# A decode step of cached attention and a gated feed-forward: VectorE transposes keys and probabilities in 32x32 blocks, and w_down becomes one plain transfer

## The chip, the cores and the metric

The kernel runs on one core of a Trainium2 chip. TensorE (PE in the profile; PEld is its weight load) does the matmuls, VectorE (DVE), ScalarE (ACT) and GpSimd (POOL) the elementwise work, and SyncE (SP) issues nearly all transfers; 16 DMA engines carry them from HBM to the on-chip memory (SBUF). Matmuls write to PSUM. The metric is the device time of one execution in microseconds; three runs of the kernel before took 231.56 to 231.65 us, median 231.6.

## The reference

A parallel block for one new token in two sequences (B = 2). The layer norm of `x` feeds grouped-query attention over the last 4096 cached positions and a gated feed-forward; both are added to `x`.

```python
xn = _layernorm(x)                                   # x: 2 x 1 x 512
# attention: 32 query heads, 8 key heads (rep = 4), Dh = 128, W = 4096
q = (xn @ wq).reshape(B, 1, 32, 128)                 # wq: 512 x 4096
k, v = k_cache[:, :, Sk - W:, :], v_cache[:, :, Sk - W:, :]
p = softmax(q . k * Dh ** -0.5)                      # each key head for 4 query heads
attn = (p @ v).reshape(B, 1, 4096) @ wo              # wo: 4096 x 512
# feed-forward, F = 1792
gate, up = xn @ W_gate, xn @ W_up
gate = gate * (gate > 0)
return x + attn + (gate * up) @ W_down
```

All is float32. The two caches give 64 MiB of keys and values; with the weights 94.9 MB are read.

## The kernel before

The work is cut into groups g = 0 to 3 (two sets of four key heads times two sequences). A group has two `k` tiles and two `v` tiles, a = 0 and 1. A tile (`load_kv`, L114) holds two heads: 64 runs of 64 positions for each, so that partition 2 p + h has run p of head h, and 64 x 128 numbers lie in a partition, 4 MiB in all. Tiles and weights share a ring of four buffers (`ring`, L59). SyncE issues loads in program order, and each waits until the load four places ahead has been used up: `wq` in two parts, `w_gate`, `w_up`, then `k0_0`, `k0_1`, `k1_0`, `v0_0`, `k1_1`, `v0_1` and so on, at the end `v3_0`, `v3_1`, `w_down`, `wo` in two halves, the second in four pieces.

At the start x is normalised, q is computed in `q_ps`, transposed and put into `qz` (L143), which is zero but for the columns of the head that a matmul is for. Gate and up follow (`g_ps`, `u_ps`; the last 128 of 1792 columns in `x_ps`), and their product goes transposed into `hT`.

For a `k` tile, `transposes` (L308) turns 64 blocks of 128x128 on TensorE. Four land in one PSUM tile `pk`, and VectorE and ScalarE by turns copy it into `kT`, even and odd partitions (the two heads) apart. `scores` (L322) is eight matmuls a half tile, of 512 columns with 32 query columns each, over four 32-column groups of the array. `softmax` (L335) finds one maximum a head (reduction on VectorE, transpose on TensorE, reduction, and a matmul that spreads the negative maximum as the bias `nm`), takes the exponential on ScalarE into `p`, with each column twice, transposes `p` on TensorE (`pp`) and masks it into `pt`. `values` (L386) multiplies `pt` with a `v` tile into `o`; `gather` (L404) picks each head's part with four matmuls into `oa`; `finish` scales by the reciprocal sum `rl`. `spread_heads` puts heads in the layout `oT` for `wo`.

The order on each engine is the order of the program text; no scheduler changes it. `kwork` (L432) writes the transposes of the next tile between the steps of `softmax`, which is a generator for that, and holds scores back by half a tile (`pend`).

At the end, `project` (L478) multiplies rows of `w_down` and `wo` with `hT` and `oT`, four matmuls of 128 columns a row, one for each quarter of the output, all accumulating in `y_ps`. `w_down` (L95) comes as 13 rows a partition in one transfer, and the 128 rows left over as two transfers to 16 partitions each (`wx`), after POOL has cleared that tile.

Of the kernel before, what the change touches and what calls it, by code (L numbers as in the profile page):

```python
# [9 lines left out]
F32 = mybir.dt.float32  # L10
# [10 lines left out]
def kernel(  # L21
# [28 lines left out]
    S1 = W // (Q * 512)  # L50

# [10 lines left out]
    ps_kt = ctx.enter_context(tc.tile_pool(name="ps_kt", bufs=3, space=PSUM))  # L62
# [23 lines left out]
    FM = 13  # L86
    KX = 4
    LEFT = 0
    FX = F - P * FM
    RX = (FX - 8 * LEFT) // (8 * KX)  # L90
    SX = RX + (LEFT > 0)
    MQ = P * FM // Q
    assert 8 * KX * RX + 8 * LEFT == FX

    def load_down():  # L95
        t = ring.tile([P, FM, D], F32, name="wd", tag="ring")
        wx = ktp.tile([P, SX, D], F32, name="wx", tag="kT")
        nc.gpsimd.memset(wx[0:64], 0.0)  # L98
        nc.sync.dma_start(
            t.rearrange("p k e -> p (k e)"), w_down[0:P * FM, :].rearrange("(p k) e -> p (k e)", p=P)  # L100
        )
        row = P * FM
        for b in range(2):
            src = bass.AP(
                tensor=w_down.tensor, offset=w_down.offset + row * D,
                ap=[[RX * D, KX], [KX * RX * D, 4], [1, RX * D]],
            )
            nc.sync.dma_start(wx[32 * b:32 * b + 4 * KX, 0:RX].rearrange("p k e -> p (k e)"), src)
            row += 4 * KX * RX
        for i in range(LEFT):  # L110
            nc.sync.dma_start(wx[i:32:4, RX], w_down[row + 8 * i:row + 8 * i + 8, :])
        return t, wx
# [21 lines left out]
    for c0, c1 in ((0, 256), (256, 384), (384, 512)):  # L134
        nc.scalar.dma_start(x2[:, c0:c1], x[:, 0, c0:c1])  # L135
# [4 lines left out]

    NSLOT = C * S1
    qz = const.tile([P, NG, NSLOT * 36], F32, name="qz")
    nc.gpsimd.memset(qz, 0.0)  # L143
    ones = const.tile([1, 1], F32, name="ones")
# [4 lines left out]
    hT = const.tile([P, FM + SX, B, 16], F32, name="hT")  # L149
    nc.gpsimd.memset(hT, 0.0)  # L150
    hx = const.tile([32, SX, 64], F32, name="hx")
    nc.gpsimd.memset(hx, 0.0)
# [10 lines left out]
    for e in range(NE):  # L163
# [3 lines left out]
    pick = const.tile([P, 4, 24], F32, name="pick")  # L167
    nc.gpsimd.memset(pick, 0.0)
    nc.vector.tensor_reduce(
        out=pick[:, :, 8:16], in_=ident.rearrange("p (q u k) -> p u k q", q=Q, u=4), op=ALU.add, axis=AX.X  # L170
    )


    HK = 2 * REP
    by_h = const.tile([P, NP, HK], F32, name="by_h")
    nc.vector.tensor_reduce(
        out=by_h, in_=ident.rearrange("p (q a s k) -> p a k q s", q=Q, a=NP, s=S1), op=ALU.add, axis=AX.XY
    )

    half_of = const.tile([P, 2], F32, name="half_of")  # L180
    nc.vector.tensor_reduce(
        out=half_of, in_=ident.rearrange("p (y h) -> p h y", h=2), op=ALU.add, axis=AX.X
    )
    own = const.tile([P, 2, REP], F32, name="own")
    nc.vector.tensor_copy(own, half_of[:, :, None].to_broadcast([P, 2, REP]))
# [42 lines left out]
    for r in range(R):  # L228
# [3 lines left out]
        for i in range(REP):  # L232
            nc.tensor.transpose(
                qt[:, i].rearrange("p c s b -> p (c s b)"), qs[:, i * P:(i + 1) * P], ident
            )
        for b in range(B):
            dst = qz[:, r * B + b].rearrange("p (a s h k) -> p a s h k", a=NP, s=S1, h=2)
            for h in range(2):
                nc.vector.tensor_copy(
                    dst[:, :, :, h, 0:REP], qt[:, :, h::2, 0:S1, b].rearrange("p i a s -> p a s i")  # L240
                )
# [4 lines left out]
    x_ps = ps_1.tile([32, 2, FX], F32, name="x_ps", tag="o0")  # L246
    for h, dst, wt in ((0, g_ps, gw), (1, u_ps, uw)):
# [6 lines left out]
        for kc in range(KC):  # L254
            nc.tensor.matmul(
                x_ps[:, h], xnT[:, 1, kc, :], wt[:, kc, Q * MQ:], start=(kc == 0), stop=(kc == KC - 1)
            )
# [8 lines left out]
    )  # L266
    gx = work.tile([32, 2, FX], F32, name="gx", tag="qs")
    nc.scalar.copy(gx[:, 0], x_ps[:, 0])
    nc.vector.scalar_tensor_tensor(gx[:, 1], gx[:, 0], 0.0, gx[:, 0], op0=ALU.is_gt, op1=ALU.mult)
    part = 4 * KX * RX  # L270
    for b in range(2):
        g_in, u_in = (
            a[:, b * part:(b + 1) * part].rearrange("p (j e s) -> p e j s", j=4, e=KX) for a in (gx[:, 1], x_ps[:, 1])
        )
        nc.vector.tensor_tensor(
            hx[:, 0:RX, 32 * b:32 * b + 4 * KX].rearrange("p s (e j) -> p e j s", j=4), g_in, u_in, op=ALU.mult
        )
    for i in range(LEFT):
        lo = 2 * part + 8 * i
        nc.vector.tensor_tensor(  # L280
            hx[:, RX, i:32:4], gx[:, 1, lo:lo + 8], x_ps[:, 1, lo:lo + 8], op=ALU.mult
        )
    ht_ps = ps_1.tile([P, FM + SX, B], F32, name="ht_ps", tag="misc")
    for k in range(FM):
        for c in range(Q):
            nc.tensor.matmul(
                ht_ps[32 * c:32 * c + 32, k], hh[:, k], ident[:, 32 * c:32 * c + B], start=True, stop=True
            )
    for k in range(SX):
        m = 64 if k < RX else 32  # L290
        nc.tensor.matmul(ht_ps[0:m, FM + k], hx[:, k, 0:m], ident[0:32, 0:B], start=True, stop=True)
    nc.vector.tensor_copy(hT[:, 0:FM, :, 0], ht_ps[:, 0:FM])
    nc.vector.tensor_copy(hT[0:64, FM:FM + RX, :, 0], ht_ps[0:64, FM:FM + RX])
    if LEFT:
        nc.vector.tensor_copy(hT[0:32, FM + RX, :, 0], ht_ps[0:32, FM + RX])

    HW = W // S1
    ss, pts, rls = {}, {}, {}  # L300
    kts, osb = {}, {}
    turn = [0]

    def evacuate(dst, src):
        (nc.vector.tensor_copy if turn[0] % 2 else nc.scalar.copy)(dst, src)  # L305
        turn[0] += 1

    def transposes(g, a, s1, kt_in):  # L308

        kt = ktp.tile([P, 2, HW], F32, name=f"kT{g}_{a}_{s1}", tag="kT")  # L310
        kts[g, a, s1] = kt
        for n in range(2 * Q):
            pk = ps_kt.tile([P, 512], F32, name=f"pk{g}_{a}_{s1}_{n}", tag="kt")
            for u in range(4):
                j = 8 * Q * s1 + 4 * n + u
                nc.tensor.transpose(pk[:, u * P:(u + 1) * P], kt_in[:, j * P:(j + 1) * P], ident)  # L316
            evacuate(
                kt[:, :, n * 256:(n + 1) * 256], pk.rearrange("p (y h) -> p h y", h=2),
            )
            yield  # L320

    def scores(g, a, s1):  # L322
        if (a, s1) == (0, 0):
            ss[g] = ps_s.tile([P, 512], F32, name=f"s{g}", tag="s")
        kt = kts.pop((g, a, s1))
        for h in range(2):
            n = (a * S1 + s1) * 2 + h
            for q in range(Q):
                nc.tensor.matmul(  # L329
                    ss[g][32 * q:32 * q + 32, :], qz[:, g, 32 * n:32 * n + 32],  # L330
                    kt[:, h, q * 512:(q + 1) * 512],
                    start=(a == 0 and s1 == 0 and h == 0), stop=(a == NP - 1 and s1 == S1 - 1 and h == 1),
                )

    def softmax(g):  # L335
# [3 lines left out]
        yield  # L339
        mt = ps_1.tile([1, P], F32, name=f"mt{g}", tag="misc")  # L340
        nc.tensor.transpose(mt, m, ident)
        mx = work.tile([1, NP, HK], F32, name=f"mx{g}", tag="mx")
        nc.vector.tensor_reduce(
            out=mx, in_=mt.rearrange("p (q a s k) -> p a k q s", q=Q, a=NP, s=S1), op=ALU.max, axis=AX.XY
        )
        mb = work.tile([1, NP, S1, HK], F32, name=f"mb{g}", tag="mb")
        nc.vector.tensor_scalar(
            mb, mx[:, :, None, :].to_broadcast([1, NP, S1, HK]), -SCALE, None, op0=ALU.mult
        )
        yield  # L350
        nm_ps = ps_1.tile([P, 1], F32, name=f"nm_ps{g}", tag="misc")
        for q in range(Q):
            nc.tensor.matmul(
                nm_ps[32 * q:32 * q + 32, :], mb.rearrange("p a s k -> p (a s k)"), ones, start=True, stop=True
            )
        nm = work.tile([P, 1], F32, name=f"nm{g}", tag="nm")
        nc.vector.tensor_copy(nm, nm_ps)  # L357

        p = work.tile([P, 512, 2], F32, name=f"p{g}", tag="p", bufs=1)
        l = work.tile([P, 1], F32, name=f"l{g}", tag="l")  # L360
        both = ss[g][:, :, None].to_broadcast([P, 512, 2])
        nc.scalar.activation(p, both, AF.Exp, bias=nm, scale=SCALE, accum_out=l)  # L362
        yield
        yield
        yield

        pts[g] = work.tile([P, 2, Q * NP * S1, 4, HK], F32, name=f"pt{g}", tag="pt")
        pv = p.rearrange("r y h -> r (y h)")
# [163 lines left out]
```

## Time and profile before

| quantity | value |
|---|---|
| median of three runs | 231.6 us (231.56 to 231.65) |
| profiled execution | 231.43 us |
| its span, first to last instruction | 229.6 us |
| mean granted TensorE clock | 0.938 of full |
| read from HBM | 94.90 MB, 413 GB/s over the span |
| TensorE busy | 81%, 1876 matmul issues |
| VectorE busy | 29%, 135 instructions |

A float32 matmul appears as two issues with a weight load each; a transpose as one. In the page, a group's row has line, engine, operation, tile written and tiles read, shape and count; then busy us, mean ns of one; then idle time before and what ended it. In the chain of waits, each piece has start, length and what it was. A stretch of the table by windows has start and end, its length, busy time (and count) of PE, PEld, DVE, ACT and POOL, then the granted clock, the DMA share and GB/s. PE busy time counts pipelined matmuls from issue to end, so it isn't the share of the array's peak.

### The profile page before, as it was taken

How to read it: one execution, taken by the hardware profiler on the slowest of the kernel's cores; microseconds unless marked ns; L12 is line 12 of the kernel's file. 1: busy time of each engine (PE TensorE's matmuls, PEld its weight loads, DVE VectorE, ACT ScalarE, POOL GpSimd, SP SyncE). 2: the span in 40 equal slices, each digit the busy share in tenths (PEclk: the TensorE clock that was granted, in tenths of full speed). 3: DMA queues.
4: the chain of work that ended last, by engine and by line, in shares of the span. 5: the costliest groups of instructions: out<-in, count | busy, mean ns of one | idle time of the engine just before them, and what ended most of it. 6: DMA issues, size and time to landing. Idle time of an engine off the chain costs nothing.

```text
span 229.6 us, 4149 instructions
## 1 busy us (share of the span) xinstructions
PE 185.4 (81%) x1876; PEld 114.7 (50%) x1876; DVE 67.2 (29%) x135; ACT 46.9 (20%) x80; POOL 8.2 (4%) x25
## 2 busy tenths in 40 slices
PE   0059961779999899997799699889979973988794
PEld 0052231259666583663484566458446532247682
DVE  0320021034444570441472143157124224001000
ACT  0020100004344451440351233045023202010000
POOL 8100000000000000000000000000000300000000
PEclk9999999577999999999999799999999999599678
DMA  7999999999999999999999999999999999999981
GB/s 274 451 428 408 454 410 437 422 451 442 405 425 451 415 417 445 442 411 420 457 417 432 428 440 414 434 445 414 422 440 437 417 428 440 423 442 414 410 364 49
DMA packets 3824, 95.15 MB, mean 414 GB/s; under 512 B 434, under 2 KB 448, under 8 KB 704
## 3 DMA queue, kind: packets, MB, share of 16 engines
q1 hardware_dynamic: 3796, 94.90, 96.7%
q8 instruction: 14, 0.23, 0.4%
q14 instruction: 2, 0.02, 0.0%
q10 hardware_dynamic: 12, 0.00, 0.0%
HBM read 94.90 MB, written 0.00 MB: 413 GB/s over the span
## 4 chain that ended last, share of the span: by engine, by line
DMA 54%; PE 41%; DVE 2%; issue 1%; ACT 1%; ACTq 0%; POOL 0%; DVEq 0%
DMA k<-in_A_k_cache_dram 37%; PE pk L316 21%; DMA wo<-in_A_wo_dram 13%; PE s L329 7%; PE y_ps L480 5%; DMA x<-in_A_x_dram 4%; PE o L393 3%; PE q_ps L222 3%; PE xt_ps L212 2%; ACT p L362 1%; PE pp L373 0%; ACTq L135 0%; PE oa L409 0%; DVE stats L189 0%; DVE kT L305 0%
## 5 line engine op out<-in xcount | busy, mean ns | idle before, releaser
L316 PE MATMUL pk<-ident,k 128*128 128x128 f32 x512 | 67.9, 286 | 6.0 <-DMA k<-in_A_k_cache_dram 5.9
L316 PEld LDWEIGHTS pk<-ident,k 128*128 128x128 f32 x512 | 57.9, 146 | 20.9 <-issue 16.7
L305 DVE COPY kT<-pk 128x512 f32<-128x512 f32 x64 | 44.2, 691 | 52.1 <-PE pk L316 46.2
L305 ACT COPY kT<-pk 128x512 f32<-128x512 f32 x64 | 37.5, 585 | 69.5 <-PE pk L316 69.5
L393 PE MATMUL o<-v,pt 128*32 128x512 f32 x256 | 32.5, 641 | 0.0
L329 PE MATMUL s<-kT,qz 128*32 128x512 f32 x256 | 30.9, 598 | 0.0
L393 PEld LDWEIGHTS o<-v,pt 128*32 128x32 f32 x256 | 11.3, 117 | 15.7 <-issue 10.9
L212 PE MATMUL xt_ps<-rep,xn 2*128 2x32 f32 x16 | 3.7, 400 | 13.9 <-DVE xn L206 13.9
L329 PEld LDWEIGHTS s<-kT,qz 128*32 128x32 f32 x256 | 7.1, 109 | 11.9 <-issue 11.5
L305 DVE COPY on<-o 128x512 f32<-128x512 f32 x4 | 2.8, 692 | 30.5 <-PE o L393 30.5
L409 PE MATMUL oa<-on,pick 128*16 128x128 f32 x64 | 8.3, 273 | 4.1 <-DVE on L305 3.3
L480 PE MATMUL y_ps<-wo,oT 128*17 128x128 f32 x256 | 10.3, 329 | 1.6 <-DMA wo<-in_A_wo_dram 1.6
L409 PEld LDWEIGHTS oa<-on,pick 128*16 128x16 f32 x64 | 5.8, 97 | 11.3 <-DVE on L305 7.0
L250 PE MATMUL u_ps<-wu,xnT 128*32 128x416 f32 x32 | 5.8, 901 | 6.1 <-DMA wu<-in_B_W_up_dram 6.1
L212 PEld LDWEIGHTS xt_ps<-rep,xn 2*128 2x128 f32 x16 | 3.6, 320 | 13.9 <-issue 13.9
L222 PE MATMUL q_ps<-wq,xnT 128*32 128x512 f32 x64 | 9.7, 777 | 0.5 <-DVE xnT L214 0.5
L480 PEld LDWEIGHTS y_ps<-wo,oT 128*17 128x17 f32 x256 | 8.1, 119 | 3.6 <-DMA wo<-in_A_wo_dram 2.6
L305 ACT COPY on<-o 128x512 f32<-128x512 f32 x4 | 2.3, 586 | 27.0 <-PE o L393 27.0
L98 POOL MEMSET wx<- 64x2048 f32 x1 | 1.8, 1804 | 169.1 <-PE s L329 169.1
L362 ACT ACTIVATE p<-s,nm 128x1024 f32<-128x1024 f32 x4 | 4.5, 1114 | 13.1 <-DVE nm L357 13.1
L374 DVE TENSOR_TENSOR pt<-pp,own 128x512 f32<-128x512 f32 x8 | 5.4, 689 | 2.6 <-PE pp L373 2.6
L373 PE MATMUL pp<-ident,p 128*128 128x128 f32 x32 | 4.9, 280 | 1.7 <-ACT p L362 1.5
(83 smaller groups left out, 68.2 us busy)
## 6 DMA issues: line engine op xcount, KB each, us to landing
k<-in_A_k_cache_dram SPq DMA_DIRECT2D x8, 4096.0 KB, 23.9
v<-in_A_v_cache_dram SPq DMA_DIRECT2D x8, 4096.0 KB, 28.3
wq<-in_A_wq_dram SPq DMA_DIRECT2D x2, 4096.0 KB, 21.7
wo<-in_A_wo_dram SPq DMA_DIRECT2D x1, 4096.0 KB
wg<-in_B_W_gate_dram SPq DMA_DIRECT2D x1, 3584.0 KB, 29.8
wu<-in_B_W_up_dram SPq DMA_DIRECT2D x1, 3584.0 KB, 39.3
wd<-in_B_W_down_dram SPq DMA_DIRECT2D x1, 3328.0 KB
wo<-in_A_wo_dram SPq DMA_DIRECT2D x1, 2048.0 KB
```

Source lines behind the costliest of these rows:

```text
L212: nc.tensor.matmul(xt_ps[:, o, kc, :], cols, rep.rearrange("r s b -> r (s b)"), start=True, stop=True)
L222: nc.tensor.matmul(q_ps[r][32 * c:32 * c + 32, :], xnT[:, 0, kc, :], wqt[kc // 2][:, kc % 2, n * 512:(n + 1) * 512], start=(kc == 0), stop ...
L250: nc.tensor.matmul(dst[32 * c:32 * c + 32, :], xnT[:, 1, kc, :], wt[:, kc, c * MQ:(c + 1) * MQ], start=(kc == 0), stop=(kc == KC - 1),)
L305: (nc.vector.tensor_copy if turn[0] % 2 else nc.scalar.copy)(dst, src)
L316: nc.tensor.transpose(pk[:, u * P:(u + 1) * P], kt_in[:, j * P:(j + 1) * P], ident)
L329: nc.tensor.matmul(ss[g][32 * q:32 * q + 32, :], qz[:, g, 32 * n:32 * n + 32], kt[:, h, q * 512:(q + 1) * 512], start=(a == 0 and s1 == 0 ...
L362: nc.scalar.activation(p, both, AF.Exp, bias=nm, scale=SCALE, accum_out=l)
L373: nc.tensor.transpose(pp[:, u], pv[:, lo:lo + P], ident)
L374: nc.vector.tensor_tensor(pts[g][:, jh].rearrange("p n u k -> p u n k"), pp.rearrange("p u (n k) -> p u n k", k=HK), own.rearrange("p h i ...
L393: nc.tensor.matmul(o[32 * q:32 * q + 32, :], pts[g][:, jh, n].rearrange("p u k -> p (u k)"), v[:, lo:lo + 512], start=(s1 == 0 and jh == 0 ...
L409: nc.tensor.matmul(oa[g], pick[:, u, 8 - 8 * a:24 - 8 * a], ons[a][:, u], start=(a == 0 and u == 0), stop=(a == NP - 1 and u == 3),)
L480: nc.tensor.matmul(y_ps[32 * e:32 * e + 17, :], lhsT.rearrange("p b s -> p (b s)")[:, 0:17], w[:, e * P:(e + 1) * P], start=False, stop=stop,)
```

## The change

Keys are no longer transposed on TensorE. VectorE's block transpose turns each 32x32 block of a `k` tile where it stands, four instructions of 2048 columns a tile, from SBUF to SBUF. A head's 128 dimensions then come as four column blocks (`CB`), with 32 partitions for 32 rows, and the four partition blocks (`PB`) hold different positions. q is therefore block diagonal: `spot` copies a block of q to all partition blocks, and sixteen small copies a set, on VectorE and ScalarE, place it in `qz`. Scores are eight matmuls a half tile as before, but a half tile's go to two of the four 32-row parts of `s`. The heads of a tile are now a and a + 2.

`p` has 512 columns, each once. A matmul with a permutation (`perm`, one for each head of a tile) reorders its rows into `pp`, and one VectorE block transpose writes `pt`. `values` copies its result through a `mask` on VectorE, so that `gather` is one matmul of 512 columns, and `finish` adds four parts.

No tile's work is written between another's steps: a step is scores, maximum, values, softmax, gather, and the turning of `p`. At the end the rows of `w_down`, `wo0` and the first eight of `wo1` are one matmul of 512 columns each, over four column groups by turns, into `y4`; that is copied and folded into `y_ps`, and the last eight rows go as before. `w_down` is one transfer with 14 rows a partition. x comes in five pieces in place of three.

```diff
+    L = 32
+    PB = P // L
+    CB = DH // L
-    ps_kt = ctx.enter_context(tc.tile_pool(name="ps_kt", bufs=3, space=PSUM))
+    ps_kt = ctx.enter_context(tc.tile_pool(name="ps_kt", bufs=2, space=PSUM))
...
     def load_down():
         t = ring.tile([P, FM, D], F32, name="wd", tag="ring")
-        wx = ktp.tile([P, SX, D], F32, name="wx", tag="kT")
-        nc.gpsimd.memset(wx[0:64], 0.0)
...
+            t.rearrange("p k e -> p (k e)"), w_down.rearrange("(p k) e -> p (k e)", p=P)
+        )
+        return t
...
-        base = cache[b, r * C + 2 * a, SK - W:SK, :]
+        base = cache[b, r * C + a, SK - W:SK, :]
-            tensor=cache.tensor, offset=base.offset, ap=[[run, PK], [SK * DH, 2], [1, run]]
+            tensor=cache.tensor, offset=base.offset, ap=[[run, PK], [NP * SK * DH, 2], [1, run]]
...
-    for c0, c1 in ((0, 256), (256, 384), (384, 512)):
+    for c0, c1 in ((0, 256), (256, 320), (320, 384), (384, 448), (448, 512)):
...
+        for cb in range(CB):
+            nc.tensor.matmul(
+                rq[:, cb].rearrange("p b c i -> p (b c i)"), spot[:, cb].rearrange("p b e -> p (b e)"),
+                qT.rearrange("p b c i -> p (b c i)"), start=True, stop=True,
+            )
         for b in range(B):
+            for pb in range(PB):
+                rows = slice(L * pb, L * pb + L)
+                for a in range(NP):
+                    lo = 2 * a * 16 + pb * REP
+                    (nc.vector.tensor_copy if a else nc.scalar.copy)(
+                        qz[rows, r * B + b, :, :, lo:lo + REP], rq[rows, :, b, a::NP, :]
+                    )
...
+    def scores(g, a, kt_in):
+        if a == 0:
             ss[g] = ps_s.tile([P, 512], F32, name=f"s{g}", tag="s")
+        for s1 in range(S1):
+            kt = ktp.tile([P, CB, 2, JH, KL], F32, name=f"kT{g}_{a}_{s1}", tag="kT")
+            for n in range(2):
+                lo = JH // 2 * n
+                j = JH * s1 + lo
+                nc.vector.transpose(
+                    kt[:, :, :, lo:lo + JH // 2, :].rearrange("p c h j k -> p j c k h"),
+                    kt_in[:, j * DH:(j + JH // 2) * DH],
                 )
+            for cb in range(CB):
+                for h in range(2):
+                    lo = 32 * (2 * s1 + h)
+                    nc.tensor.matmul(
+                        ss[g][lo:lo + 32, :], qz[:, g, cb, h, 16 * a:16 * a + 32],
+                        kt[:, cb, h].rearrange("p j k -> p (j k)"),
+                        start=(a == 0 and cb == 0), stop=(a == NP - 1 and cb == CB - 1),
+                    )
...
+    def turn(g, p, l):
+        pp = ps_kt.tile([P, 2, 512], F32, name=f"pp{g}", tag="kt")
+        for h in range(2):
+            nc.tensor.matmul(pp[:, h], perm[:, h], p, start=True, stop=True)
+        pts[g] = work.tile([P, NP * S1, JH, HK], F32, name=f"pt{g}", tag="pt")
+        nc.vector.transpose(pts[g].rearrange("p n j k -> p j n k"), pp.rearrange("p h y -> p y h"))
...
+    for g in range(NG):
         for a in range(NP):
             kt_in = load_kv(k_cache, "k", g, a)
+            v_in = load_kv(v_cache, "v", g - 1, a) if g else None
+            scores(g, a, kt_in)
+            nm = maxima(g) if a else None
+            if g:
+                values(g - 1, a, v_in)
+            pl = softmax(g, nm) if a else None
+            if g:
+                gather(g - 1, a)
+                if a:
+                    finish(g - 1)
+                elif g % B == 1 and g > 1:
+                    spread_heads((g - 2) // B)
             if a:
+                turn(g, *pl)
...
+    def slot(lhsT, w):
+        t, i = done[0] % Q, done[0]
+        nc.tensor.matmul(
+            y4[32 * t:32 * t + 32, :], lhsT.rearrange("p b s -> p (b s)"), w, start=(i < Q), stop=(i >= EARLY - Q)
+        )
+        done[0] += 1
...
+            if j == cuts[1][1]:
+                ys = work.tile([P, D], F32, name="ys", tag="qs")
+                nc.vector.tensor_copy(ys, y4)
+                quarters(fold[:, 0:17], ys, False)
```

Three places show how instructions moved. A row has the line, the operation, the tile written (with group and a in its name), the tiles read, the shape and how many in a row. The first is VectorE between the scores of group 1 and the first tile of group 2. Before:

```order
L305 COPY kT1_1_1_788<-pk1_1_1_4_813 128x2x256
L305 COPY kT1_1_1_788<-pk1_1_1_6_825 128x2x256
L305 COPY on0_1_867<-o0_1_850 128x512
L418 TENSOR_SCALAR osb0_873<-oa0_845,rl0_673 16x128
L305 COPY kT2_0_0_879<-pk2_0_0_1_886 128x2x256
L338 TENSOR_REDUCE m1_906<-s1_699 128x1
L305 COPY kT2_0_0_879<-pk2_0_0_3_908 128x2x256
L343 TENSOR_REDUCE mx1_916<-mt1_914 1x16
```

The same place now:

```order
L294 STREAM_TRANSPOSE kT1_1_1_461<-k1_1_446 128x16x4x16x2 x2
L310 TENSOR_REDUCE m1_472<-s1_402 128x1
L314 TENSOR_REDUCE mx1_476<-mt1_474 1x16
L319 TENSOR_SCALAR mb1_478<-mx1_476 1x64 x2
L325 COPY nm1_483<-nm_ps1_481 128x1
L357 TENSOR_TENSOR on0_1_502<-o0_1_485,mask_120 128x512
L374 TENSOR_REDUCE su0_509<-oa0_444 16x128
L375 TENSOR_SCALAR osb0_508<-su0_509,rl0_396 16x128
L339 STREAM_TRANSPOSE pt1_515<-pp1_512 128x32x4x8
L343 RECIPROCAL rl1_519<-lp1_517 16x1
L294 STREAM_TRANSPOSE kT2_0_0_526<-k2_0_521 128x16x4x16x2 x2
```

The first tile of group 2 stood ahead of the maximum of group 1; now it stands behind the whole softmax of group 1 and the masked results `on` of the tile before.

On TensorE, the same group, before:

```order
L329 MATMUL s1_699<-kT1_1_0_731,qz_91 32x512 x8
L409 MATMUL oa0_845<-on0_0_725,pick_118 16x128 x4
L393 MATMUL o0_1_850<-v0_1_729,pt0_633 32x512 x16
L409 MATMUL oa0_845<-on0_1_867,pick_118 16x128 x4
L316 MATMUL pk2_0_0_0_880<-ident_86,k2_0_875 128x128 x4
L316 MATMUL pk2_0_0_1_886<-ident_86,k2_0_875 128x128 x4
L329 MATMUL s1_699<-kT1_1_1_788,qz_91 32x512 x8
```

And now:

```order
L301 MATMUL s1_402<-kT1_1_0_450,qz_93 32x512 x8
L301 MATMUL s1_402<-kT1_1_1_461,qz_93 32x512 x8
L312 MATMUL mt1_474<-ident_88,m1_472 1x128
L323 MATMUL nm_ps1_481<-ones_97,mb1_478 128x1
L352 MATMUL o0_1_485<-v0_1_448,pt0_392 32x512 x16
L365 MATMUL oa0_444<-on0_1_502,picks_124 16x512
L337 MATMUL pp1_512<-p1_504,perm_132 128x512 x2
```

The `pk` transposes, 64 a tile, are gone, and with them the work that stood between one step's results and the next.

The last place is TensorE's end, after the last `values`. Before:

```order
L480 MATMUL y_ps_1579<-wd_1538,hT_97 17x128 x52
L480 MATMUL y_ps_1579<-wx_1539,hT_97 17x128 x16
L423 MATMUL op1_1701<-osb1_1524,spread_108 128x32 x8
L480 MATMUL y_ps_1579<-wo0_1711,oT_101 17x128 x64
L480 MATMUL y_ps_1579<-wo1_1777,oT_101 17x128 x64
```

Now:

```order
L424 MATMUL y4_788<-wd_780,hT_101 32x512 x14
L380 MATMUL op1_847<-osb1_763,spread_110 128x32 x8
L424 MATMUL y4_788<-wo0_857,oT_103 32x512 x16
L424 MATMUL y4_788<-wo1_875,oT_103 32x512 x8
L431 MATMUL y_ps_782<-ys_888,fold_128 17x128 x4
L431 MATMUL y_ps_782<-wo1_875,oT_103 17x128 x32
```

One matmul of 512 columns stands where four of 128 stood, for all but the last eight rows of `wo`, and the fold stands between.

More of the change, by code (lines that the diff above doesn't have):

```diff
@@ L266 @@
     )
[L267 to L277, printed above, removed]
@@ L292 @@
[L292 to L295, printed above, removed]
+    ht_ps = ps_1.tile([32, FM * Q, B], F32, name="ht_ps", tag="misc")
+    firsts = ident.rearrange("p (c r) -> p c r", c=Q)[:, :, 0:B]
+    for k in range(FM):
+        nc.tensor.matmul(ht_ps[:, k * Q:(k + 1) * Q], hh[:, k], firsts, start=True, stop=True)
+    for c in range(Q):
+        nc.vector.tensor_copy(hT[32 * c:32 * c + 32, :, :, 0], ht_ps[:, c::Q])
@@ L299 @@
     HW = W // S1
+    JH = J // S1
+    KL = L // 2
     ss, pts, rls = {}, {}, {}
[L301 to L320, printed above, removed]
@@ L345, in softmax @@
         )
[L346 to L350, printed above, removed]
+        mb = work.tile([1, S1, C, PB, REP], F32, name=f"mb{g}", tag="mb")
+        for s1 in range(S1):
+            nc.vector.tensor_scalar(
+                mb[:, s1], mx[:, :, None, :].to_broadcast([1, C, PB, REP]), -SCALE, None, op0=ALU.mult
+            )
         nm_ps = ps_1.tile([P, 1], F32, name=f"nm_ps{g}", tag="misc")
[L352 to L355, printed above, removed]
+        nc.tensor.matmul(nm_ps, mb.rearrange("p s x b i -> p (s x b i)"), ones, start=True, stop=True)
@@ L364, in softmax @@
[L364 to L368, printed above, removed]
[L369 to L378 removed]
+        nc.scalar.activation(p, ss[g], AF.Exp, bias=nm, scale=SCALE, accum_out=l)
```

210 lines of the change are left out of this document (70 added, 140 removed).

## The prediction

> **What bounds the kernel now.** I read the page's slices first, then the table by stretches, then the chain of waits, and last the timeline around the places that the change rewrites.
>
> ```profile
> PE 185.4 (81%) x1876; PEld 114.7 (50%) x1876; DVE 67.2 (29%) x135; ACT 46.9 (20%) x80; POOL 8.2 (4%) x25
> DMA  7999999999999999999999999999999999999981
> q8 instruction: 14, 0.23, 0.4%
> ...
> 120.00:140.00 20.00, 17.93 (x142) 11.72 (x141) 6.87 (x12) 5.82 (x10) 0.00 (x0) 0.91 1.01 430
> ...
> 220.00:224.00 4.00, 4.00 (x128) 3.62 (x120) 0.00 (x0) 0.00 (x0) 0.00 (x0) 0.81 0.85 348
> 224.00:227.00 3.00, 2.56 (x76) 1.49 (x64) 0.29 (x1) 0.00 (x0) 0.00 (x0) 1.00 0.21 82
> ```
>
> The DMA row is full from the second slice to the last but one, and the stretch 120 to 140 moves 430 GB/s with all engines busy. PE at 81% looks close to a bound, but it is fed by the transfers: the chain steps from a matmul back to a landing again and again.
>
> ```profile
> 24.50 26.72 DMA k<-in_A_k_cache_dram
> 100.73 28.26 DMA k<-in_A_k_cache_dram
> 129.12 5.48 PE pk L316 x32
> 136.46 3.97 PE pk L316 x32
> 216.27 7.96 PE y_ps L480 x189
> 224.27 1.29 PE y_ps L480 x40
> 226.20 0.46 PE y_ps L480 x8
> 226.69 0.29 DVE yo L502
> ```
>
> The first `k` tile lands at 24.50 + 26.72 = 51.22 us, the sixth `k` tile at 128.99. Eight transfers of 4096 KB lie between: (128.99 - 51.22) / 8 = **9.72 us each**, 38.9 us for the four tiles of a group (two of `k`, two of `v`). So the kernel now runs as fast as data come; whatever the engines save inside the loop is worth nothing by itself. What can be gained lies after the last landing and in the ragged end of the transfers; what can be lost is a loop whose own length exceeds 38.9 us.
>
> **Is the new loop shorter than 38.9 us?** The old code interleaves `k` transposes of the next group with softmax, so no engine waits long. The new order is serial: VectorE transposes a `k` tile, TensorE multiplies, VectorE masks the result of `values`, and only then come the transposes of the next tile. I add up one group, from rows.
>
> ```profile
> L305 DVE COPY kT<-pk 128x512 f32<-128x512 f32 x64 | 44.2, 691 | 52.1 <-PE pk L316 46.2 <-ACT on L305 5.2
> L214 DVE COPY xnT<-xt_ps 128x256 f32<-128x256 f32 x1 | 0.4, 423 | 3.9 <-PE xt_ps L212 3.9
> L338 DVE TENSOR_REDUCE m<-s 128x1 f32<-128x512 f32 x4 | 2.8, 691 | 4.8 <-PE s L329 4.8
> L347 DVE TENSOR_SCALAR mb<-mx 1x32 f32<-1x32 f32 x4 | 0.7, 169 | 0.1
> 60.33 1.85 PE s L329 x16
> 195.47 6.37 PE L393 MATMUL o<-v,pt 128*32 128x512 f32 x32
> 189.19 0.69 DVE L338 TENSOR_REDUCE m<-s 128x1 f32<-128x512 f32 x1 [1.43 <-PE s L329]
> 191.36 1.11 ACT L362 ACTIVATE p<-s,nm 128x1024 f32<-128x1024 f32 x1 [11.38 <-DVE nm L357]
> 87.49 3.43 PE o L393 x32
> ```
>
> A *VectorE transpose* has no row. Two copies give the price of a column: (691 - 423) / 256 = 1.05 ns, with 155 ns fixed. A transpose of 128x2048 at one column a step is then 2048 x 1.05 + 155 = **2.30 us**. Below, two columns a step would make it 1.2 us; above, a transpose that passes each column twice would make it 4.4 us. I take 2.30, the row of the same engine, type and kind of work; the ends are rivals below.
> The Trainium skill speaks against that value: its page "VectorE: DVE Perf Modes", section "The three transpose paths", states 311 ns for a 128x128 bf16 block set. Sixteen such sets would be 4.98 us by it. No row of this trace shows a transpose on VectorE, so by that figure the third rival holds.
>
> *Scores*: a half tile was 16 issues (eight matmuls, two issues each) over four column groups of 32 in 1.85 us. One round of 512 columns takes 0.43 us (3.43 us for 32 issues of `o`, eight rounds of four). The new `scores` writes rows 32 (2 s1 + h), so only two groups work at a time: 16 issues are eight rounds and a drain, 3.6 us. The first half runs beside transposes three and four (4.6 us); the second half follows them. *Values*: `o`, 32 issues over four groups, 3.43 us and its drain, 3.6; with the masked copy (0.69, as the copies of 128x512 above) and hops, 4.5.
>
> - Step a = 0: four transposes 9.2, second half of scores 3.6, values and mask 4.5: **17.3 us**.
> - Step a = 1: 9.2 + 3.6; maximum to bias 191.36 - 189.19 = 2.17, with one more `mb` of 0.17, 2.35; values and mask 4.5; `oa`, two issues of 512 columns in one group, 0.86; the permutation `pp`, four full-width issues of 0.43, 1.72; its transpose of 1024 columns 1.23; hops 0.4: **23.9 us**. ACT's exponential lies beside `values`.
>
> That is 41.2 us at full clock, already 2.3 us over 38.9. The clock will not stay full. TensorE idles through the first two transposes of each step (4.6 us). Before, 32 `pk` issues took 5.48 us after a wait for `k`, against 3.97 us in the run that followed: 1.5 us lost, and the stretch 120 to 140 has a granted clock of 0.91. The `o` issues of 195.47 took 6.37 us instead of 3.6, 2.8 us lost. Between these, 2.15 us a step, of which 1.0 (4.6 - 3.6) is covered by transposes three and four: 1.15 a step, 2.3 a group. The gap in softmax (2.35 us) may cost another 0 to 2.8 us; I take nothing. **43.5 us a group.**
> The Trainium skill's page "TensorE: Matmul & The Clock Gate", Part 1, says that the clock halves after about one idle window of 3.4 us and returns after such a window of sustained work. By it the 4.6 us gaps cool the array and the softmax gap need not. The trace agrees on the halving and the order of the loss (1.5 and 2.8 us), though the wait at 129.12 was shorter than a window.
>
> **The sum to the end.** The second `k` tile lands at 51.22 + 9.72 = 60.9. Its transposes, scores with the cold start, bias, exponential (0.8), `pp`, transpose and hops are 9.2 + 4.75 + 2.35 + 0.8 + 1.7 + 1.2 + 0.5 = 20.5, so group 0 is done at 81.5. Three groups of 43.5 end at 212.0. Behind that stand, all with data landed:
>
> ```profile
> L480 PE MATMUL y_ps<-wd,hT 128*17 128x128 f32 x104 | 3.2, 273 | 0.0
> L423 PE MATMUL op<-osb,spread 16*128 16x32 f32 x32 | 3.9, 273 | 0.0
> ```
>
> Two `values` with mask and gather, 2 x (4.5 + 0.86) = 10.7; `wd` as 28 issues of 512 columns at 1.85 / 16 = 0.116 us, 3.25; `op` and its copy 2.25; `wo0` and the first eight rows of `wo1`, 48 issues, 5.55; the copy `ys` 0.9; `fold` and the last 64 issues, 72 at 3.2 / 104 = 0.03 us, 2.2; drain 0.3. In sum 25.1: `yo` starts at 237.1, against 226.69. From there the ends are alike (229.6 - 226.69 = 2.9): a span of 240.0. The profiled execution took 231.43 us beside its span of 229.6, 1.83 more, and the runs' median is 231.6: **241.7 us, say 241.5**.
>
> **Transfers in that picture.** A tile is loaded when the tile four loads earlier is used up, so the lag becomes late issues.
>
> ```profile
> 179.39 0.33 SPq L99 DMA_DIRECT2D wd<-in_B_W_down_dram  x1
> 185.58 18.08 SPq L498 DMA_DIRECT2D wo<-in_A_wo_dram  x5
> 1.58 8.89 DMA x<-in_A_x_dram
> wu<-in_B_W_up_dram SPq DMA_DIRECT2D x1, 3584.0 KB, 39.3
> ```
>
> `wd` waits for the last `k` tile: 212.0 - 43.5 + 17.3 + 1.15 + 9.2 = 196, 17 us later than now; `wo0` waits for `o` behind it, at 207. By then the queue has just run dry (two further tiles and `wd` are due at about 207), so `wo0` lands near 219 and `wo1`, issued at 216, near 229. TensorE reaches them at 228 and 232: late, but not what decides. The rest costs nothing while this holds. The plain `wd` (3584 KB in one transfer) replaces 3328 KB, two small transfers and POOL's memset in the same queue; the 128 KB pieces went away from where the queue is full. Two more pieces of `x` may double the 8.89 us wait of the layer norm, and sixteen small copies of `qz` add some 3 us before the gate matmuls; cover: loads are in flight until `wu` lands at 2.15 + 39.3 = 41.5, and the first `k` is not needed before 51.2. Fewer TensorE issues (1876 to 948) mean about 7 instruction packets instead of 14.
>
> **The rivals.**
>
> 1. *The transfers stay the bound* (the other side). If the loop is under about 40 us (a transpose nearer 2.0 us, or a clock that stays up), the lag never reaches the end: with three groups of L, `yo` starts at 81.5 + 3 L + 25.1, which meets today's 226.69 at L = 40.0. Then the end is the last landing. The ragged end (348 and 82 GB/s in 7 us, some 1.4 MB under the full rate, 3 us) can shrink with half the instruction packets and a balanced `wd`; I take 0.3 to 1.2 us of it, 230.6 us. For it speaks the full DMA row, against it the sum of 41.2 us without any cold start. Chance 0.20.
> 2. *Two column groups don't lift the clock.* Every warm-up in the trace came with four groups or full width. If two are too few, both score halves run at half rate, 7.2 us each: a step grows from 9.2 + 3.6 to 4.6 + 14.4, by 6.2, and cold `o` adds up to 2.8. L is 53.6 to 59; with 56, 87 + 168 + 25 + 2.9 + 1.83 = 285 us. Against it: nothing shows the clock counting groups. Chance 0.08.
> 3. *A transpose passes each column twice* (4.4 us). Eight a group add 17, and hide the cold starts: L = 58; with 9 more ahead, 90 + 174 + 25 + 2.9 + 1.83 = 294 us. Chance 0.04.
>
> **How the numbers follow.** The forecast has 0.68. Its own range: L moves by 8 us per us of transpose, and 2.15 to 2.5 us, with 0 to 2.8 for the softmax gap, gives 236 to 250. The first rival joins below, so the range is 230.4 to 250; the two dear rivals (0.12) are left out. A measurement of this kernel tells 0.2%, about 0.5 us, from no change. Of the first rival's 0.20 some 0.16 is faster by more than that and 0.04 within it; all else is slower, 0.80.
>
> **What would show it.** Right: 32 transposes near 2.3 us; VectorE busy near 100 us; a granted clock well under 0.94, low at the start of each score block; `k` issues drifting later by 4 to 5 us a group against their landings; DMA digits under 9 only in the last fifth; the chain alternating between VectorE transposes, `s` and `o`, with hardly any DMA at its end. Wrong: transposes of 1.2 or 4.4 us; `s` in 1.85 or 7 us; or a chain that still ends on `wo`, which is the first rival.

## The result, and the profile after

The changed kernel takes 278.69 us (median of six runs, 277.64 to 281.30), the kernel before 231.48 us (231.28 to 231.65) beside it: a ratio of 1.206, with a 95% interval of 1.199 to 1.213. The forecast was slower, but 241.5 us. The profiled execution took 277.64 us, with a span of 275.9 us. So the loss is 47 us and not 10.

From the page of the changed kernel: busy time, two rows of the slices, the instruction queue, and the chain that ended last, by engine and by line.

```profile
PE 166.6 (60%) x948; PEld 51.7 (19%) x948; DVE 147.2 (53%) x121; ACT 8.3 (3%) x27; POOL 8.1 (3%) x31
...
PEclk9999968859898559959995797799759957999999
DMA  7999999999999905996996289799907992999940
...
q8 instruction: 7, 0.11, 0.2%
...
DVE 48%; PE 41%; issue 6%; POOL 3%; ACT 1%; POOLq 0%; ACTq 0%
DVE kT L294 40%; PE o L352 10%; PE s L301 9%; PE q_ps L221 3%; PE pp L337 3%; PE y L424 3%; PE oa L365 2%; DVE pt L339 2%; PE g_ps L258 2%; DVE on L357 2%; PE op L380 1%; PE xt_ps L211 1%; PE u_ps L258 1%; PE rq L239 1%; DVE m L310 1%
```

The DMA row, which was full, has holes from the fifteenth slice on, and the chain, in which transfers had 54%, has none. It runs through VectorE and TensorE by turns, and 40% of the span is one line: the block transposes of the keys. TensorE is busy for 60% and VectorE for 53%. So the loop is now serial and longer than the transfers, as forecast; what differs is by how much.

The groups of instructions, with different shapes apart, show the two kinds of block transpose:

```profile
L294 DVE STREAM_TRANSPOSE kT<-k 128x2048 f32<-128x2048 f32 x32 | 115.6, 3722 | 0.0
...
L339 DVE STREAM_TRANSPOSE pt<-pp 128x1024 f32<-128x1024 f32 x4 | 5.0, 1250 | 7.0 <-PE pp L337 7.0
```

The second, of 1024 columns out of PSUM, takes 1.25 us, close to the forecast's 1.05 ns a column and 0.155 us (1.23 us). The first, of 2048 columns, should then take 2.3 us and takes 3.7 us. A group's place in the chain of waits (start, length, what):

```profile
86.75 3.21 PE pp L337 x4
...
91.27 14.39 DVE kT L294 x4
...
109.33 3.46 PE o L352 x26
...
113.42 14.48 DVE kT L294 x4
127.95 3.65 PE s L301 x16
...
133.77 3.62 PE o L352 x32
...
139.19 1.93 PE pp L337 x4
141.14 1.25 DVE pt L339
142.43 14.39 DVE kT L294 x4
...
193.59 14.38 DVE kT L294 x4
...
246.66 1.25 DVE pt L339
...
272.98 0.29 DVE yo L456
```

From 91.27 to 142.43 and from there to 193.59 are 51.16 us each, where 43.5 us were forecast. Four transposes last 14.4 us, 3.60 us from one start to the next. They last as long around 100 us, where the DMA row shows a 0, as elsewhere, so the transfers do not stretch them.

### The profile page after: what moved, and what is told of

Read it like the earlier page. It is cut to its first block, busy times and chain, and to the rows that moved or that the text cites. A ratio compares the mean times of both kernels' runs of the same rounds, so it can differ in the third digit from the quotient of the medians.

```text
span 275.9 us, 2205 instructions
## 1 busy us (share of the span) xinstructions
PE 166.6 (60%) x948; PEld 51.7 (19%) x948; DVE 147.2 (53%) x121; ACT 8.3 (3%) x27; POOL 8.1 (3%) x31
## 3 DMA queue, kind: packets, MB, share of 16 engines
q1 hardware_dynamic: 3756, 94.90, 82.2%
HBM read 94.90 MB, written 0.00 MB: 344 GB/s over the span
## 4 chain that ended last, share of the span: by engine, by line
DVE 48%; PE 41%; issue 6%; POOL 3%; ACT 1%; POOLq 0%; ACTq 0%
DVE kT L294 40%; PE o L352 10%; PE s L301 9%; PE q_ps L221 3%; PE pp L337 3%; PE y L424 3%; PE oa L365 2%; DVE pt L339 2%; PE g_ps L258 2%; DVE on L357 2%; PE op L380 1%; PE xt_ps L211 1%; PE u_ps L258 1%; PE rq L239 1%; DVE m L310 1%
## 5 line engine op out<-in xcount | busy, mean ns | idle before, releaser
L301 PE MATMUL s<-kT,qz 128*32 128x512 f32 x256 | 77.3, 760 | 66.1 <-DVE kT L294 66.1
L294 DVE STREAM_TRANSPOSE kT<-k 128x2048 f32<-128x2048 f32 x32 | 115.6, 3722 | 0.0
L301 PEld LDWEIGHTS s<-kT,qz 128*32 128x32 f32 x256 | 16.5, 134 | 122.7 <-DVE kT L294 77.7
L357 DVE TENSOR_TENSOR on<-o,mask 128x512 f32<-128x512 f32 x8 | 5.5, 692 | 40.4 <-PE o L352 40.4
L365 PE MATMUL oa<-on,picks 128*16 128x512 f32 x16 | 8.3, 597 | 6.5 <-DVE on L357 6.5
L337 PE MATMUL pp<-p,perm 128*128 128x512 f32 x16 | 9.1, 699 | 1.2 <-ACT p L331 1.2
L339 DVE STREAM_TRANSPOSE pt<-pp 128x1024 f32<-128x1024 f32 x4 | 5.0, 1250 | 7.0 <-PE pp L337 7.0
L424 PE MATMUL y<-wo,oT 128*32 128x512 f32 x48 | 5.4, 594 | 0.0
L258 PE MATMUL g_ps<-wg,xnT 128*32 128x448 f32 x32 | 4.5, 717 | 0.0
L424 PE MATMUL y<-wd,hT 128*32 128x512 f32 x28 | 4.5, 595 | 0.0
```

The source lines that it names most:

```text
L258: nc.tensor.matmul(dst[32 * c:32 * c + 32, :], xnT[:, 1, kc, :], wt[:, kc, c * MQ:(c + 1) * MQ], start=(kc == 0), stop=(kc == KC - 1),)
L294: nc.vector.transpose(kt[:, :, :, lo:lo + JH // 2, :].rearrange("p c h j k -> p j c k h"), kt_in[:, j * DH:(j + JH // 2) * DH],)
L301: nc.tensor.matmul(ss[g][lo:lo + 32, :], qz[:, g, cb, h, 16 * a:16 * a + 32], kt[:, cb, h].rearrange("p j k -> p (j k)"), start=(a == 0 an ...
L337: nc.tensor.matmul(pp[:, h], perm[:, h], p, start=True, stop=True)
L339: nc.vector.transpose(pts[g].rearrange("p n j k -> p j n k"), pp.rearrange("p h y -> p y h"))
L357: nc.vector.tensor_tensor(ons[a], o.rearrange("p (u d) -> p u d", u=4), mask[:, :, None].to_broadcast([P, 4, P]), op=ALU.mult)
```

## The experiments

Theory W: the k transposes are slow because of the order in which they write. The output is seen as `p c h j k` and written in the order `p j c k h`, so that neighbours of one block row land 2 KB apart; pt's transpose writes runs of eight. Rivals: the source in SBUF is slow (S), or the loop around the transposes stretches them (L).

**Transposes by themselves.** Two `k` tiles are loaded, and then VectorE alone runs transposes and copies, four of each. The comments give the lines of the kernel; not shown are the loops of four, the preparing copies, a transpose of 1024 columns and one in order into `po`, in PSUM (L139):

```diff
+    far = t.rearrange("p (c h j k) -> p j c k h", c=4, h=2, j=16)
+    near = t.rearrange("p (c j h k) -> p j c k h", c=4, h=2, j=16)
+    runs = t.rearrange("p (c j k h) -> p j c k h", c=4, h=2, j=16)
+    nc.vector.transpose(t, k0)                    # L121
+    nc.vector.transpose(runs, k0)                 # L123
+    nc.vector.transpose(near, k0)                 # L125
+    nc.vector.transpose(far, k0)                  # L127, the changed kernel's
+    nc.vector.transpose(t[:, 0:128], k0[:, 0:128])    # L131
+    nc.vector.transpose(t, ps)                    # L135, ps in PSUM
+    nc.vector.transpose(far, ps)                  # L137
+    nc.vector.tensor_copy(t, k0)                  # L141
+    nc.vector.tensor_copy(far, blk)               # L143, blk = k0 by blocks
+    nc.vector.tensor_copy(far, pso)               # L145, pso = ps by blocks
```

> Leaves the whole computation out: after two k tiles have landed, VectorE alone runs, four times each, transposes and copies of 128x2048 that differ in one thing: where they read and in which order they write. Theory W (the write pattern of the k transposes, neighbours 2 KB apart, sets their 3.6 us): 3.6 us with that pattern from SBUF and from PSUM alike, and 2.3 us (2048 columns at the 1.07 ns of pt's transpose, and 0.15) with contiguous writes or with runs of 32; a copy with the same scattered write is slow too. Theory S (a source in SBUF is slow): 3.6 us for every transpose out of SBUF, 2.3 us out of PSUM. Theory L (the loop around them, transfers or TensorE, stretched them): all 2.3 us here, the scattered one too. A pattern that writes each block on a contiguous 128 bytes but with its pairs 64 bytes apart tells whether distance or order counts: 2.3 us if only distance does, 3.6 us if order does.

Its groups of instructions:

```profile
L127 DVE STREAM_TRANSPOSE t<-k 128x2048 f32<-128x2048 f32 x4 | 14.9, 3732 | 0.1
L137 DVE STREAM_TRANSPOSE t<-ps 128x2048 f32<-128x2048 f32 x4 | 14.8, 3704 | 0.1
L145 DVE COPY t<-ps 128x2048 f32<-128x2048 f32 x4 | 14.7, 3678 | 0.1
L125 DVE STREAM_TRANSPOSE t<-k 128x2048 f32<-128x2048 f32 x4 | 14.5, 3636 | 0.1
L139 DVE STREAM_TRANSPOSE po<-k 128x2048 f32<-128x2048 f32 x4 | 9.3, 2330 | 0.1
L135 DVE STREAM_TRANSPOSE t<-ps 128x2048 f32<-128x2048 f32 x4 | 9.3, 2316 | 0.1
L121 DVE STREAM_TRANSPOSE t<-k 128x2048 f32<-128x2048 f32 x4 | 9.2, 2312 | 0.1
L123 DVE STREAM_TRANSPOSE t<-k 128x2048 f32<-128x2048 f32 x4 | 9.2, 2312 | 0.1
...
L143 DVE COPY t<-k 128x2048 f32<-128x2048 f32 x4 | 7.9, 1968 | 0.1
L141 DVE COPY t<-k 128x2048 f32<-128x2048 f32 x4 | 4.9, 1222 | 0.1
L131 DVE STREAM_TRANSPOSE t<-k 128x128 f32<-128x128 f32 x4 | 1.2, 311 | 0.1
```

W holds and both rivals fall. With nothing else at work, the kernel's pattern takes 3.73 us out of SBUF and 3.70 us out of PSUM; in order the same transpose takes 2.31 us out of SBUF and 2.32 us out of PSUM, and in runs of 32, out of SBUF, 2.31 us. Pairs 64 bytes apart cost nearly the same as pairs 2 KB apart (3.64 us), so distance isn't it. It isn't the transpose either: a copy out of PSUM with that write takes 3.68 us.

**How long a run must be.** Again VectorE alone, four of each, shown without the loops:

```diff
+    r1, r2, r4, r8 = (
+        t.rearrange("p (b h k r) -> p b k h r", h=2, k=16 // r, r=r) for r in (1, 2, 4, 8)
+    )
+    nc.vector.transpose(r1, k0)                   # L125; r2, r4, r8: L127, L129, L131
+    nc.vector.transpose(every, k0)                # L133, every second column written
+    nc.vector.transpose(every4, k0[:, 0:1024])    # L135, every fourth
+    nc.vector.transpose(po.rearrange("p (b h k) -> p b k h", h=2, k=16), k0)  # L137, PSUM
```

> Leaves the whole computation out: VectorE alone, four times each, transposes of 128x2048 whose writes alternate between two places 64 bytes apart or less in runs of 1, 2, 4 and 8 columns, writes that go up in steps of 8 and of 16 bytes, and the same alternation into PSUM. Theory A (a write costs more when it finds no neighbour in the same 16 bytes): runs of 1 take 3.6 us; runs of 2, 4, 8 and steps of 8 bytes 2.3 us; steps of 16 bytes, 1024 columns, 1.8 us instead of 1.25 us. Theory B (every write that does not follow its neighbour costs 0.65 ns more): runs of 2 take 3.0 us, of 4 2.6 us, of 8 2.5 us, steps of 8 bytes 3.6 us. Into PSUM: 3.6 us if the VectorE itself is slow on such an order, 2.3 us if the SBUF is.

```profile
L125 DVE STREAM_TRANSPOSE t<-k 128x2048 f32<-128x2048 f32 x4 | 14.4, 3595 | 0.1
L137 DVE STREAM_TRANSPOSE po<-k 128x2048 f32<-128x2048 f32 x4 | 9.3, 2331 | 0.1
L127 DVE STREAM_TRANSPOSE t<-k 128x2048 f32<-128x2048 f32 x4 | 9.2, 2312 | 0.1
...
L133 DVE STREAM_TRANSPOSE t<-k 128x2048 f32<-128x2048 f32 x4 | 9.2, 2302 | 0.1
...
L135 DVE STREAM_TRANSPOSE t<-k 128x1024 f32<-128x1024 f32 x4 | 7.9, 1979 | 0.1
```

Theory A holds and B falls: runs of two are enough (2.31 us), steps of 8 bytes are free (2.30 us), steps of 16 bytes are not (1.98 us for 1024 columns, where 1.25 us is the price in order; 1.8 us was expected). A write is slow when it shares its 16 bytes of SBUF with no neighbour in time. Into PSUM the alternation is free (2.33 us, and 2.33 us in order). The Trainium skill states this rule on its page "SBUF — State Buffer", section "Specifications (TRN2)": lines of 16 bytes, at least two hits a line for full bandwidth, and a penalty for each cross to a new one. These rows agree on the two hits and give the size, 0.63 to 0.71 ns a column; a cross alone, after two hits, shows no penalty (runs of two and steps of 8 bytes).

**The write order alone, in the kernel.** The scores then read every second column:

```diff
-            kt = ktp.tile([P, CB, 2, JH, KL], F32, name=f"kT{g}_{a}_{s1}", tag="kT")
+            kt = ktp.tile([P, CB, JH, KL, 2], F32, name=f"kT{g}_{a}_{s1}", tag="kT")
...
-                    kt[:, :, :, lo:lo + JH // 2, :].rearrange("p c h j k -> p j c k h"),
+                    kt[:, :, lo:lo + JH // 2].rearrange("p c j k h -> p j c k h"),
...
-                        kt[:, cb, h].rearrange("p j k -> p (j k)"),
+                        kt[:, cb, :, :, h].rearrange("p j k -> p (j k)"),
```

> The changed kernel, but the k transposes write runs of 32 contiguous columns, and the scores read every second column instead. Theory W: transposes of 2.3 us, 1.3 us less each, so a group of 51.2 us becomes 51.2 - 8 x 1.3 = 40.8 us at full clock, and up to 43.5 us if the cold clock shows again as forecast; 241 us in all with the forecast's loss of clock, 234 us without any. Theories S and L: transposes stay at 3.6 us and the time at 278 us. If the strided read costs TensorE something, the 16 issues of a half of the scores take over 3.65 us at full clock.

It takes 241.13 us (four runs, 238.46 to 241.81), 1.041 times the kernel before (1.036 to 1.046). From its groups, and its chain of waits:

```profile
L294 DVE STREAM_TRANSPOSE kT<-k 128x2048 f32<-128x2048 f32 x32 | 71.0, 2273 | 1.9 <-PE s L301 1.9
```

```profile
84.33 4.41 DVE kT L294 x2
...
101.09 4.50 DVE kT L294 x2
105.64 8.22 PE s L301 x32
...
116.03 5.31 PE o L352 x32
...
126.38 4.42 DVE kT L294 x2
...
158.15 3.62 PE o L352 x32
...
166.80 4.41 DVE kT L294 x2
...
201.76 5.31 PE o L352 x32
...
210.82 1.25 DVE pt L339
```

The transposes are at 2.27 us, and 37.6 us of the 47.2 us lost are back. The groups last 42.0, 40.4 and (to the end of the last `pt`, 212.1) 45.3 us. The time is the forecast's, within 0.4 us, but in part by luck, as the account of the prediction below shows. Theory W holds in the kernel, and S and L fall once more. The strided read costs little: by the starts of single matmuls in the trace a round of scores takes 0.45 us at full clock, against 0.43 us in the changed kernel.

**The order alone.** The slow transposes stay, but two of the next tile stand ahead of this one's softmax, and one ahead of `pt`:

```diff
+        flip(t, 1, 1)
+        scores(g, a)
+        if g:
+            o = values(g - 1, a, v_in)
+        if t + 1 < NT:
+            flip(t + 1, 0, 0)
+            flip(t + 1, 0, 1)
+        m = row_max(g) if a else None
+        if g:
+            masked(g - 1, a, o)
+        nm = maxima(g, m) if a else None
```

Shown is the middle of a step. `flip` is one transpose, by tile and quarter; `masked` is the copy through `mask`, taken out of `values`, and `row_max` the first reduction of `maxima`.

> The changed kernel with its slow transposes as they are, but the order on VectorE changed: the first two transposes of the next k tile stand ahead of the mask and the softmax of this one, the third ahead of pt's, so that TensorE multiplies while VectorE transposes. Theory O (the serial order makes the loop 51 us): a group is VectorE's own work, 8 x 3.62 + 2 x 0.69 + 0.69 + 0.28 + 0.36 + 0.16 + 0.95 + 1.36 and some waits, 35 to 37 us, under the 38.9 us of the transfers; the transfers are the bound again and the time is 231 to 234 us. Rival (the units are slowed by each other, by the clock or by memory, and not by waiting): the transposes lengthen or the scores stay cold, a group stays over 42 us and the time over 240 us.

It takes 239.25 us (238.16 to 239.98), 1.033 times the kernel before (1.031 to 1.036): over the range expected by 5 us. Its DMA row, and VectorE in order of time (start, length, what):

```profile
DMA  7999999999999999299999999999999999999930
```

```profile
52.23 36.06 DVE L294 STREAM_TRANSPOSE kT<-k 128x2048 f32<-128x2048 f32 x10
...
95.48 1.25 DVE L349 STREAM_TRANSPOSE pt<-pp 128x1024 f32<-128x1024 f32 x1 [1.09 <-PE pp L345]
...
108.31 14.75 DVE L294 STREAM_TRANSPOSE kT<-k 128x2048 f32<-128x2048 f32 x4
...
146.22 14.77 DVE L294 STREAM_TRANSPOSE kT<-k 128x2048 f32<-128x2048 f32 x4
```

A group is 37.9 us (108.31 to 146.22), a little over the 35 to 37 us expected but under the transfers' 38.9 us: for the loop, Theory O holds. But the first three tiles that arrive are all `k`: VectorE needs 14.5 us for each, a transfer 9.7 us, and from 52.23 on it transposes ten times without a pause. The ring fills, and one slice of the DMA row falls to 2. The `pt` of group 0 ends at 96.7 us; three groups of 37.9 us and the 25.1 us that follow the last `pt` make 235.5 us, and `yo` starts at 235.31. So the late first group accounts for the excess. That it has no `v` tiles between its `k` tiles was missing from the expectation.

**Both.**

> The changed kernel with both edits together: k transposes that write runs of 32 columns, and the next tile's transposes ahead of this one's softmax. Theory W with O: VectorE needs 8 x 2.3 + 4.8 = 23 to 26 us a group, TensorE about 30 us, both under the 38.9 us of the transfers, and a tile's four transposes (9.2 us) are now shorter than a tile's transfer (9.7 us), so the transfers do not wait in the first group either, as they did with 3.7 us each: the end is the last landing again, 230.5 to 232 us, within 0.5 us of the kernel before. Rival (shorter waits leave TensorE's cold clock as the next bound): over 234 us, with a DMA row that has gaps.

It takes 230.11 us (five runs, 229.98 to 230.26), 0.994 times the kernel before (0.993 to 0.996): a little faster than the kernel before, by 0.6%, and a little below the range expected. From its page, with the row of the last `wo` piece from its transfers (KB, us from issue to landing):

```profile
DMA  7999999999999999999999999999999999999991
...
q8 instruction: 7, 0.11, 0.2%
...
DMA 50%; PE 23%; DVE 18%; issue 4%; POOL 3%; ACT 1%; POOLq 0%; DVEq 0%; ACTq 0%
```

```profile
wo<-in_A_wo_dram SPq DMA_DIRECT2D x1, 256.0 KB, 22.2
```

and the same row of the kernel before:

```profile
wo<-in_A_wo_dram SPq DMA_DIRECT2D x1, 256.0 KB, 22.9
```

The transfers are the bound again. The last one, issued at 202.76, lands at 224.97 us; in the kernel before it was issued at 203.24 and landed at 226.16 us. The 0.53 us from there to `yo` are the same, so the gain of 1.1 us lies in the transfers, though both kernels read 94.90 MB.

**Is it the instruction queue?** Into each step of that kernel go 50 matmuls of one element, whose result is not used:

```diff
+        pad = ps_1.tile([1, 1], F32, name=f"pad{t}", tag="misc")
+        for _ in range(50):
+            nc.tensor.matmul(pad, ones, ones, start=True, stop=True)
```

> The kernel with both edits, and in each of the eight steps 50 matmuls of one element by one element, whose result nobody reads: 800 issues more, as many weight loads, 100 KB of instructions or about six packets more in the instruction queue, and some 2 to 4 us of TensorE a step, under the transfers. Theory P (the kernel with both edits ends 1.1 us before the old one because its instruction queue moves 7 packets and not 14): 12 to 14 packets, and 0.5 to 1.1 us more than without them, 230.6 to 231.2 us. Rival (the gain is elsewhere, in the order of the last loads or at the end): 12 to 14 packets and 229.9 to 230.4 us, as without them. Over 231.5 us the added matmuls themselves would be in the way, and nothing could be said.

It takes 232.22 us (231.57 to 233.45), 1.004 times the kernel before (1.003 to 1.006): over the bound from which it was to say nothing. From the page, the groups and the transfers:

```profile
DMA  7999999999999999999999999999999999999970
...
q8 instruction: 13, 0.21, 0.4%
```

```profile
L416 PE MATMUL pad<-ones 1*1 1x1 f32 x800 | 21.1, 158 | 0.0
```

```profile
wo<-in_A_wo_dram SPq DMA_DIRECT2D x1, 256.0 KB, 18.0
```

The added matmuls got in the way. One part can still be read: the last landing came at 226.36 us (issued at 208.40), 1.39 us later than without them, with 13 packets instead of 7. The data packets of each trace (queue q1), added up by their ends, tell more: the first 70 MB had landed at 166.56 us in the kernel before, at 165.76 us with both edits, at 166.51 us with the added matmuls, and at 166.14 us in the run with `w_down` alone, below, which has 14 instruction packets. So the lead of 0.8 us is there long before the last loads are issued, and it is gone with 13 packets; but half of it also appears with 14, in another execution. This fits the instruction packets and does not show them: the cause of the 1.1 us stays open.

**w_down alone**, in the kernel before:

```diff
-    FM = 13
...
+    FM = F // P
...
-        wx = ktp.tile([P, SX, D], F32, name="wx", tag="kT")
-        nc.gpsimd.memset(wx[0:64], 0.0)
...
-            t.rearrange("p k e -> p (k e)"), w_down[0:P * FM, :].rearrange("(p k) e -> p (k e)", p=P)
+            t.rearrange("p k e -> p (k e)"), w_down.rearrange("(p k) e -> p (k e)", p=P)
```

> The kernel before with only the second part of the change: w_down as one plain transfer of 14 rows a partition. As forecast the edit has no cost where the queue is full, and the two small transfers that go away took 1.25 us on four of the 16 engines: 230.8 to 231.6 us against 231.5 us. Rival: the 256 KB that move into the big transfer, and the wider gate matmuls, cost more than that, 231.8 to 232.5 us.

It takes 231.41 us (11 runs) beside 231.24 us (15 runs): a ratio of 1.0007 (0.9998 to 1.0016), inside the first range and no difference that can be told.

## Why the prediction was wrong, step by step

The path that the forecast described is the path that was measured, VectorE and TensorE by turns. The step that failed is one term of its sum, the price of a transpose, of which eight stand in a group.

- **The price of a VectorE transpose.** The sum took 2.30 us from the columns of two copies. That is right for a transpose that writes in order or in runs (2.31 us alone, 2.27 us in the kernel), but not for this one, whose rearrangement in the diff writes single columns by turns to two places: 3.60 us from start to start. The step looked at type, size and engine and left the write pattern out. The bounds of 1.2 and 4.4 us held it; the forecast's own range reached only to 2.5 us. That range is also added up wrongly: 8 x 0.2 and 2.8 us more in each of three groups, and 4 x 0.2 in the first, lead to 255.5 us and not to 250; the measured time lies outside either.
- **What the wrong price did.** Eight transposes a group at 1.30 us more are 10.4 us, so 41.2 us without any loss of clock become 51.6 us; 51.16 us were measured. In the first group the first tile's transposes now outlast the second tile's landing: 50.87 + 4 x 3.6 = 65.3 us instead of 60.9 us. That and four dearer transposes are 9.6 us, and `pt` ended at 91.2 us instead of 81.5 us. Two errors cancel inside: the last scores of the group took 3.65 us where 4.75 stood, and `pp` 3.21 us where 1.7 stood, at a granted clock of 0.59.
- **The other terms of the group held.** A half of the scores on two column groups took 3.65 us at full clock (3.6 forecast); from the end of the transposes to the next tile, step a = 1 took 142.43 - 127.95 = 14.5 us (14.7 forecast); from the last `pt` to `yo` 25.1 us passed (25.1 forecast).
- **The cold clock cost the loop nothing here**, where 2.3 us a group were forecast. The cold first half of the scores hides behind transposes three and four, which now last 7.2 us. With transposes of 2.27 us the term was oversized too: 32 issues took 8.22 us against 2 x 3.65 = 7.3 us, a loss of 0.9 us and not 2.15 us, and nearly all of it was covered: the scores ended 12.8 us after the first transpose began (101.09 to 113.86), where four transposes and a warm half are 9.0 + 3.65 = 12.65 us. The gap in softmax, taken as nothing, did cost 1.7 us there (`o` in 5.31 us instead of 3.62 us, with a granted clock of 0.50 from 116.8 to 120.2), in two groups of three.
- **One term was forgotten**: `spread_heads` in the last group, about 3 us (193.59 to 247.9 is 54.3 us instead of 51.2 us). So the forecast's 241.5 us, against 241.13 us with the transposes at their forecast price, holds partly because errors cancel, which is luck: group 0 ended 2.8 us late there, and three groups took 127.8 us instead of 130.5 us.
- **The rivals.** The first, transfers as the bound below a loop of 40.0 us, at 230.6 us, wasn't this kernel, but its condition is confirmed: with the loop shortened the time is 230.11 us. The second falls: with nothing but scores on two column groups at work, the granted clock was 0.50 from 120.7 to 124.9 us and 1.00 from there to 126.4 us, and a round went from 0.85 to 0.43 us. The third had the right place, a dearer transpose, but neither its mechanism nor its size. The Trainium skill's figure that stood beside it ("VectorE: DVE Perf Modes", section "The three transpose paths", 311 ns for a 128x128 set) agrees with the 311 ns of 128 columns alone, here in float32. But such a short one contains the fixed time: 2048 columns in order take 2.31 us, so sixteen of them, 4.98 us, are no price for one long transpose.
- **Edits costed at nothing** were free where it was tried: `w_down` alone changed nothing measurable. The five pieces of `x` and the copies into `qz` weren't tried apart, and their cover was thinner than forecast: the layer norm began at 14.06 us instead of 10.60, the gate matmuls at 40.36 us instead of 31.56, and the first transposes stood right behind `hT`, at 50.87 us. Little can be lost by that, as the tile landed at 51.22 us in the kernel before. But in the kernel with only the write order mended they began at 52.57 us; this and cold scores, which held the two `kT` buffers, put off the second tile's transposes to 63.34 us, where 60.9 was forecast, and so made most of the 2.8 us.

So the 47 us have two causes, and most of the loss needs both: transposes that write badly, and an order in which nothing stands beside them. Mending either alone brings back 37.6 or 39.4 us and leaves 8 to 10 us over the kernel before; mending both brings back 48.6 us.

## What to carry to other kernels

Read the write pattern of every rearranged output before pricing the instruction: a pattern into SBUF whose innermost step goes to another 16 bytes each time cost VectorE half as much again in the float32 transposes here, and a layout with runs of two float32 columns avoids it. When work moves to an engine that was idle, add up the serial chain of a step and not the engine's load, and put the next tile's share of that work where this tile's chain would wait. Where loads of one kind come in a row at the start, price the loop for that stretch by itself.

## What was unexpected of the hardware

- VectorE writes to PSUM are indifferent to the alternation that costs 55% into SBUF: 2.33 us against 3.60 us.
- The same scattered write costs a copy out of SBUF much less than one out of PSUM: 1.97 us (1.22 us in order) against 3.68 us (2.29 us in steps of 8 bytes). No run explains this.
- TensorE reads a right-hand operand in steps of 8 bytes at 95% of its pace: 0.45 us a round of 512 columns instead of 0.43 us, both at full clock.
